# Second batch of an attention-and-Fourier kernel: q and k turned by VectorE, and the block mask added by TensorE

## The chip, the cores and the metric

The kernel runs on one core of one Trainium2 chip. A core has five engines that run their own instruction streams and wait for each other by semaphores: TensorE (matmuls; PE in the profile, its weight loads PEld), VectorE (DVE), ScalarE (ACT), GpSimd (POOL) and SyncE (SP), which here issues most of the transfers. The metric is the device time of one execution in microseconds (us), the median of several runs.

## The reference, cut to what matters

Block-sparse attention for four batches of eight heads, then a Fourier mixing and a two-layer channel network. Everything is float32.

```python
B, H, S, D = 4, 8, 768, 64            # attention
block, n_rand = 32, 3                 # 24 blocks of 32 rows
scores = scale * np.matmul(q, k.transpose(0, 1, 3, 2))
mask = np.abs(blk_i - blk_j) <= 1     # neighbours
mask = mask | first and last block (rows and columns) | three sampled blocks per block row
scores = np.where(mask, scores, -1000000000.0)
attn = softmax(scores);  attn_out = np.matmul(attn, v)
x = attn_out of all heads side by side           # (4, 768, 512)

mixed = np.real(fft(fft(x, axis=1), axis=2))     # Fourier mixing
u = x + mixed
un = (u - mean) / np.sqrt(var + 1e-06)           # per row
out = u + np.maximum(un @ w_ch1, 0.0) @ w_ch2    # channels: 512 -> 2048 -> 512
```

## The kernel before

Two heads form a pair; a batch has four pairs (NP = 4), all batches sixteen, numbered n = 0 to 15. A pair has 12 units (2 halves of the queries times 6 chunks of the keys); a slot handles 2 units, so a pair takes 6 slots and a batch 24 (SB = 24). Slots 0 to 23 are the first batch, 24 to 47 the second, 48 to 71 the third, 72 to 95 the fourth. While a batch's attention runs, the mixing and channels ("mixer") of the batch before it are put into the gaps. The order of instructions on every engine is fixed when the kernel is built, by a small model of the engines' times (`busy`, `when`); on the chip each engine works through its stream in that order.

The scores of a unit have to be masked. The first batch does it on TensorE: a second, bf16 matmul of two small factors (which key block, and which blocks are off for a query) adds a large negative number to the scores in PSUM, so that the exponential is 0. The later batches multiply by a 0/1 mask on VectorE after the exponential. Later batches also have GpSimd add up the exponentials (the row sums), where the first batch uses TensorE.

```python
def scores(us):
    ...
    for u in us:
        s = ps_s.tile([P, 2, 512], FP32, tag="s", name="s")        # 2 buffers in PSUM
        ...
            nc.tensor.matmul(s[:, i, 0:HS], kT[rows, c * P:(c + 1) * P], qT[rows, queries],
                             start=True, stop=n >= NP)
    for u, s in got if n < NP else ():                              # first batch only
        ...
            nc.tensor.matmul(s[:, i, 0:HS], of_k[rows, c * P:(c + 1) * P], off_q[rows, queries],
                             start=False, stop=True)

def weigh(u, s):
    e = ep.tile([P, 2, HS], FP32, tag="e", name="e")                # 4 buffers
    if n < NP:
        nc.scalar.activation(out=e, in_=s[:, :, 0:HS], func=ACT.Exp, scale=scale)
        return
    nc.scalar.activation(out=s[:, :, 0:HS], in_=s[:, :, 0:HS], func=ACT.Exp, scale=scale)
    nc.vector.tensor_tensor(out=e, in0=s[:, :, 0:HS], in1=m.broadcast_to([P, 2, HS]), op=ALU.mult)
    ...
    for i in range(2 if c > 0 else 0):
        nc.gpsimd.tensor_add(out=acc, in0=e_of[u - 1][:, i, :] if c == 1 else acc, in1=e[:, i, :])

def values(u):                          # one slot after its scores
    nc.tensor.matmul(o[D * i:D * i + D, :], vt[:, i, c, :], e[:, i, :], ...)
```

The score matmul needs q and k with the head's dimension on the partitions. Up to pair BY_VECTOR - 1 they are loaded row by row and turned by TensorE into PSUM, from where ScalarE copies them. From pair BY_VECTOR on they are loaded in blocks of 32x32 and turned by VectorE within the blocks; ScalarE then brings the turned q into the order that the mixer needs.

```python
BY_VECTOR = 2 * NP + 1                  # 9

def turn(n, a, half):                   # by TensorE: 6 transposes for k, 6 for q a pair
    nc.tensor.transpose(tp[:, c * P:(c + 1) * P], part, ident)
    ...                                 # then copies on ScalarE

def flip_blocks(n, a):                  # by VectorE
    nc.vector.transpose(out=out, in_=t)

def in_order(n):                        # q only: six copies on ScalarE
    nc.scalar.copy(...)

# in slot(sl), where n, s = divmod(sl, SP): the pair, and its slot from 0 to 5
if s == at and n + 1 < BY_VECTOR: short.append(... turn(n + 1, a, half))
if BY_VECTOR <= n + 1 < len(pairs):
    for at, fn, args in ((0, squares, (n + 1, 0)), (1, flip_blocks, (n + 1, 0)),
                         (2, in_order, (n + 1,)), (4, flip_blocks, (n + 1, 1)),
                         (5, squares, (n + 1, 1))): ...
```

The mixer of a batch: scale x by the row sums, fold it (VectorE), cosine and sine matmuls (zp), matmuls along the other axis (pq), add to x, mean and variance, normalise to un (VectorE), transpose un (utp, TensorE), then the channels: products xp, yp, z of the first layer and y of the second. The channels of a batch are released (`late.extend(rest)`) when everything before them has been put into the streams. In slots 53 and 77 the kernel puts out whatever of the mixer two batches back is still missing (`until`), because x of the new batch takes that batch's buffer.

```python
def begin(b):
    before, after, rest = mixer(b, x_of[b, 0], x_of[b, 1])
    apart.extend((*step, any_of) for step in norm_steps(b) + before)
    apart.extend((*step, hold) for step in after)
    apart.append(("-", lambda: late.extend(rest), 0.0, 0.0, 0.0, hold))

# the weights' raw words pass through six buffers, big0 to big5, which the mixer and
# the channels use afterwards; VectorE converts the last of 32 chunks about slot 23
def room(i, shape, name, dtype=FP32):
    return big.tile(shape, dtype, tag=f"big{i}", name=name)
```

The factors lie in the two buffers of the pool acc_p, which GpSimd's sums take over with the second batch.

Of the kernel before, what the change touches and what calls it, by code (L numbers as in the profile page):

```python
# [12 lines left out]
BF16 = mybir.dt.bfloat16  # L13
# [4 lines left out]
ALU = mybir.AluOpType  # L18
ACT = mybir.ActivationFunctionType
# [83 lines left out]
def kernel(  # L103
# [24 lines left out]
    HS = S // 2  # L128
# [7 lines left out]
    scale = 1.0 / float(D) ** 0.5  # L136
    KA = D + NB
    NP = H // 2
# [27 lines left out]
    mask = const.tile([P, C, S], U8, name="mask")  # L166
# [25 lines left out]
    def busy(engine, us, after=0.0):  # L192
        when[engine] = max(when[engine], after) + us
        return when[engine]
# [11 lines left out]
    HOP = 0.1  # L206
# [2 lines left out]
    loaded, v_of = {}, {}  # L209


    BY_VECTOR = 2 * NP + 1

    def load_blocks(n, a, tile):

# [219 lines left out]
    def room(i, shape, name, dtype=FP32):  # L435
        return big.tile(shape, dtype, tag=f"big{i}", name=name)
# [29 lines left out]

    turned, e_of, acc_of, o_of, sums_of, x_of, sp_of = {}, {}, {}, {}, {}, {}, {}
    s_at, e_at, oT_at, acc_at = {}, {}, {}, {}  # L470

# [64 lines left out]
    def scores(us):  # L536

        n, w = divmod(us[0], UP)
        half = w // C
        qT, kT = turned[n, 0], turned[n, 1]  # L540
        queries = slice(half * HS, (half + 1) * HS)
        got = []
        for u in us:
            c = u % C
            s = ps_s.tile([P, 2, 512], FP32, tag="s", name="s")
            got.append((u, s))
            busy("PE", 0.72, max(e_at.get(u - SLOT, 0.0), z_at[u % 2]))
            s_at[u] = when["PE"] + HOP
            for i in range(2):
                rows = slice(D * i, D * i + D)  # L550
                nc.tensor.matmul(s[:, i, 0:HS], kT[rows, c * P:(c + 1) * P], qT[rows, queries],  # L551
                                 start=True, stop=n >= NP)
        for u, s in got if n < NP else ():
            c = u % C
            busy("PE", 0.25)
            s_at[u] = when["PE"] + HOP
            for i in range(2):
                rows = slice(D * i, D * i + D)
                nc.tensor.matmul(s[:, i, 0:HS], of_k[rows, c * P:(c + 1) * P], off_q[rows, queries],
                                 start=False, stop=True)  # L560
        return got

    def weigh(u, s):
        n, w = divmod(u, UP)
        half, c = divmod(w, C)
        e = ep.tile([P, 2, HS], FP32, tag="e", name="e")
        e_of[u] = e
        if n < NP:
            nc.scalar.activation(out=e, in_=s[:, :, 0:HS], func=ACT.Exp, scale=scale)
            e_at[u] = busy("ACT", 0.8, s_at[u]) + HOP  # L570
            return
        nc.scalar.activation(out=s[:, :, 0:HS], in_=s[:, :, 0:HS], func=ACT.Exp, scale=scale)  # L572
        m = mask[:, c, half * HS:(half + 1) * HS].rearrange("p (o s) -> p o s", o=1)
        nc.vector.tensor_tensor(out=e, in0=s[:, :, 0:HS], in1=m.broadcast_to([P, 2, HS]),  # L574
                                op=ALU.mult)
        e_at[u] = busy("DVE", 0.97, busy("ACT", 0.8, s_at[u]) + HOP) + HOP
        if c > 0:
            acc_at[n, half] = busy("POOL", 2.0, e_at[u]) + HOP
        if c == 1:
            acc_of[n, half] = acc_p.tile([P, 2, HS], FP32, tag="acc", name="acc")  # L580

        for i in range(2 if c > 0 else 0):
            acc = acc_of[n, half][:, i, :]
            nc.gpsimd.tensor_add(out=acc, in0=e_of[u - 1][:, i, :] if c == 1 else acc,  # L584
                                 in1=e[:, i, :])
# [665 lines left out]
    def begin(b):  # L1251


        before, after, rest = mixer(b, x_of[b, 0], x_of[b, 1])
        any_of = len(late) + len(apart) + 4 * len(rest)
        hold = 2 * T
        apart.extend((*step, any_of) for step in norm_steps(b) + before)
        apart.extend((*step, hold) for step in after)
        apart.append(("-", lambda: late.extend(rest), 0.0, 0.0, 0.0, hold))

    def w_loads():
        while state["got"] < min(len(wchunks), state["w"] + ROOMS):
# [3 lines left out]
    def w_steps(sl):  # L1266
        while state["w"] < min(len(wchunks), W_PACE * sl):
            w_round(state["w"])
            state["w"] += 1

    def slot(sl):
        phase, r = divmod(sl, SB)
        n, s = divmod(sl, SP)
        units = range(SLOT * sl, SLOT * sl + SLOT)
        if sl < B * SB:
            for u, ps in scores(units):
                weigh(u, ps)
        if not late:
            gap(1.5)
        if 0 < sl <= B * SB:  # L1280
            done = [u - SLOT for u in units]
            for u in done:
                values(u)
            if phase == 0 or sl == SB:
                add_up(done)
            for u in done:
                e_of.pop(u)
        if s == 3 and n + 2 < len(pairs):
            load_q(n + 2)
        if s == 0 and 0 < n < len(pairs) - 1:  # L1290
            load_k(n + 1)

        reuse = n % NP == 0 and phase >= 2
        if sl > 0 and s == (5 if reuse else 3) and sl <= B * SB:
            b, j = pairs[n]
            at = oT_at[n, 0]
            if reuse:
                until(lambda: (b - 2, 0) in finished)
                at = when["PE"] + LEAVES
            if in_blocks(n):  # L1300
                place_blocks(n, 0)
            else:
                short.append(("t", at, lambda: place(n, 0)))
        if 0 < sl <= B * SB and s == 0 and n % NP != 1:
            if in_blocks(n - 1):
                place_blocks(n - 1, 1)
            else:
                short.append(("t", oT_at[n - 1, 1], lambda: place(n - 1, 1)))
        if sl < B * SB and n % NP == 1 and s == 1:
            b = pairs[n - 1][0]  # L1310
            at = oT_at[n - 1, 1]
            if b >= 2:
                until(lambda: (b - 2, 1) in finished)
# [12 lines left out]
        if sl == 1:  # L1326
            short.append(("t", 0.0, lambda: turn(0, 0, 1)))
        if phase == 0 and 4 <= sl < 4 + 2 * C:
            short.append(("m", 0.0, lambda: mask_step(sl - 4)))
        if r == 1 and 0 < phase:  # L1330
            begin(phase - 1)
        left = SB * (phase + (0 if r == 0 else 1)) + 1 - sl
        us = sum(step[1] for step in late)
        pace = max(LEAST, min(MOST, (us - COVER) / left)) if left > 0 else MOST
        state["owed"] = min(state["owed"], pace) + pace if late else 0.0
        gap(max(state["owed"], 0.0))
        while late and state["owed"] >= late[0][1] / 2:
            state["owed"] -= late[0][1]
            channel_step()
            gap(max(state["owed"], 0.0))  # L1340

        while short and (s in (2, 5) or len(short) > 1 or phase == 0 or r == 0):
            ready = [i for i in short if max(i[1], min(free[i[0]])) <= when["PE"] + 0.1]
            if not ready and s not in (2, 5) and r > 0 and sl > 1:
                break
            item = ready[0] if ready else short[0]
            short.remove(item)
            item[2]()
# [3 lines that stand above are left out]
                                 (5, squares, (n + 1, 1))):  # L1352
                if s == at:
                    fn(*args)
        w_loads()
        w_steps(sl)
        if sl >= 4 and sl % 2 == 0:
            table_step()

# [139 lines left out]
```

## Time and profile before

The time before is 1092.57 us (median of 3 runs, 1092.56 to 1092.97). The profiled execution has a span of 1089.3 us.

| group of instructions | count | mean |
|---|---|---|
| scores on TensorE (s, line 551) | 768 records | 523 ns |
| mask factors on TensorE (s from at_q and at_k, bf16, line 559) | 96 | 323 ns |
| exponential on ScalarE into e (line 569) and in place (line 572) | 48 and 144 | 823 and 791 ns |
| mask multiply on VectorE (e from s and mask, line 574) | 144 | 948 ns |
| sums on GpSimd (acc, line 584) | 240 | 1058 and 1055 ns |
| block transposes on VectorE, of k and of q (line 520) | 7 and 7 | 1524 and 967 ns |
| transposes of q and k on TensorE (tp, line 486) | 108 | 288 to 299 ns |

A float32 matmul shows as two records. Matmuls overlap, so the mean of one record is longer than the time by which it advances the engine; that is read from the starts in the timeline. In the 40 equal slices of the page (27.2 us each) a digit is the busy share in tenths. The second batch's attention falls into slices 5 to 9, where VectorE is at 7 to 9 tenths and GpSimd at 6 to 8:

```profile
PE   8999988988999999999999999999999999999996
...
DVE  5899887598745524664567536554556355575663
ACT  6988655555111102353342202334230302220210
POOL 1000186788000001255555000244530001000000
```

### The profile page before, as it was taken

Reading aid. Unit: us, or ns where it says so; the run is one execution under the profiler, and the core shown is the slowest. Engines: PE = TensorE matmul, PEld = TensorE weight load, DVE = VectorE, ACT = ScalarE, POOL = GpSimd, SP = SyncE. Lnnn points to the kernel's source line nnn. Section 1 sums busy time; section 2 is a strip of 40 time slices with the busy share of each in tenths; the row PEclk is TensorE's granted clock in tenths of the full one; section 3 lists DMA queues with packets and bytes.
Section 4 is the critical chain, followed back from the end, with each engine's and each line's share of the span. In section 5 each row is a group of like instructions: output and inputs, shape, how many; then the busy total and the mean of one; then the engine's idle time right before and its main releaser. Section 6 shows DMA issues by size and latency. Waiting matters only on the chain.

```text
span 1089.3 us, 12419 instructions
## 1 busy us (share of the span) xinstructions
PE 1048.1 (96%) x4334; PEld 534.4 (49%) x4334; DVE 675.3 (62%) x1241; ACT 379.1 (35%) x762; POOL 270.2 (25%) x302
## 2 busy tenths in 40 slices
PE   8999988988999999999999999999999999999996
PEld 4333333533555545443444555443344555568575
DVE  5899887598745524664567536554556355575663
ACT  6988655555111102353342202334230302220210
POOL 1000186788000001255555000244530001000000
PEclk9999999999999999999999999999999999999999
DMA  7757211121000001222311000212000001000001
GB/s 223 229 163 242 78 45 44 30 45 29 0 1 1 0 1 29 59 38 43 56 22 33 0 1 10 63 37 40 13 8 8 1 1 29 30 1 1 1 17 45
DMA packets 108194, 46.66 MB, mean 43 GB/s; under 512 B 95822, under 2 KB 100956, under 8 KB 108124
## 3 DMA queue, kind: packets, MB, share of 16 engines
q1 hardware_dynamic: 106236, 44.99, 16.2%
q10 hardware_dynamic: 1856, 0.79, 0.3%
q8 instruction: 36, 0.59, 0.2%
q14 instruction: 34, 0.28, 0.1%
q0 software_dynamic: 32, 0.01, 0.0%
HBM read 37.11 MB, written 6.29 MB: 40 GB/s over the span
## 4 chain that ended last, share of the span: by engine, by line
PE 83%; DVE 9%; ACT 3%; issue 2%; DMA 2%; POOL 1%; SPq 0%; ACTq 0%; DVEq 0%; POOLq 0%
PE y L1048 23%; PE z L992 15%; PE s L551 10%; PE o L597 8%; PE yp L992 7%; PE yy L1111 6%; PE xp L992 3%; DVE e L574 3%; PE zp L805 2%; PE sp L663 1%; PE zp L776 1%; DMA out_dram<-x 1%; DVE x L855 1%; POOL acc L584 1%; PE tp L486 1%
## 5 line engine op out<-in xcount | busy, mean ns | idle before, releaser
L584 POOL TENSOR_TENSOR acc<-acc,e 128x384 f32<-128x384 f32 x192 | 196.8, 1058 | 83.8 <-DVE e L574 83.2
L551 PE MATMUL s<-qT,kT 64*128 64x384 f32 x768 | 157.4, 523 | 13.9 <-DVE e L574 12.1
L574 DVE TENSOR_TENSOR e<-s,mask 128x768 f32<-128x768 f32 x144 | 131.1, 948 | 58.6 <-ACT s L572 53.3
L572 ACT ACTIVATE s<-s 128x768 f32<-128x768 f32 x144 | 109.6, 791 | 112.1 <-PE s L551 111.1
L597 PE MATMUL o<-e,vr 128*64 128x384 f32 x768 | 145.5, 500 | 0.0
L1051 DVE TENSOR_TENSOR x<-y,x 128x512 f32<-128x512 f32 x72 | 49.7, 690 | 139.4 <-PE y L1048 139.3
L1048 PE MATMUL y<-w_sb,hA 128*128 128x512 f32 x288 | 129.8, 597 | 1.1 <-ACT zs L807 1.1
L1048 PE MATMUL y<-w_sb,hB 128*128 128x512 f32 x288 | 128.7, 597 | 1.0 <-DVE x L1051 1.0
L551 PEld LDWEIGHTS s<-qT,kT 64*128 64x128 f32 x768 | 63.7, 187 | 89.7 <-DVE e L574 43.1
L584 POOL TENSOR_TENSOR acc<-e 128x384 f32<-128x384 f32 x48 | 49.6, 1055 | 219.6 <-DVE e L574 170.3
L997 DVE TENSOR_TENSOR hA<-z,hA 128x384 f32<-128x384 f32 x64 | 35.7, 557 | 96.3 <-PE z L992 96.3
L992 PE MATMUL z<-unT,t 128*128 128x384 f32 x256 | 93.0, 486 | 0.0
L868 POOL TENSOR_SCALAR st<-st 128x1 f32<-128x1 f32 x24 | 6.6, 276 | 347.0 <-DVE st L867 346.5
L1048 PEld LDWEIGHTS y<-w_sb,hB 128*128 128x128 f32 x288 | 53.3, 190 | 68.5 <-issue 66.5
L1048 PEld LDWEIGHTS y<-w_sb,hA 128*128 128x128 f32 x288 | 52.9, 190 | 64.8 <-issue 58.3
L597 PEld LDWEIGHTS o<-e,vr 128*64 128x64 f32 x768 | 46.8, 137 | 76.3 <-issue 71.1
L1001 ACT ACTIVATE hA<-hA 128x384 f32<-128x384 f32 x64 | 33.5, 523 | 120.1 <-DVE hA L997 119.9
L992 PEld LDWEIGHTS z<-unT,t 128*128 128x128 f32 x256 | 48.6, 190 | 33.9
L1001 ACT ACTIVATE hB<-hB 128x384 f32<-128x384 f32 x64 | 33.5, 523 | 86.3 <-DVE hB L997 86.3
L1012 ACT COPY hA<-xp 128x384 f32<-128x384 f32 x32 | 15.3, 478 | 100.0 <-PE xp L992 100.0
L992 PE MATMUL xp<-unT,w_sb 128*128 128x384 f32 x128 | 48.9, 505 | 1.3 <-DVE x L1051 0.7
L992 PE MATMUL yp<-unT,w_sb 128*128 128x384 f32 x128 | 46.9, 489 | 0.4 <-DVE un L841 0.4
(200 smaller groups left out, 1388.1 us busy)
## 6 DMA issues: line engine op xcount, KB each, us to landing
wraw<-in_moe_w_ch_dram SPq DMA_DIRECT2D x32, 512.0 KB
vr<-in_v_dram SPq DMA_DIRECT2D x30, 192.0 KB
qr<-in_q_dram SPq DMA_DIRECT2D x48, 64.0 KB
x<-oT SPq DMA_DIRECT2D x192, 12.0 KB
kr<-in_k_dram SPq DMA_DIRECT2D x14, 192.0 KB
qb<-in_q_dram SPq DMA_DIRECT2D x28, 96.0 KB
kb<-in_k_dram SPq DMA_DIRECT2D x28, 96.0 KB
out_dram<-x SPq DMA_DIRECT2D x16, 128.0 KB
```

The lines of the kernel that those rows point to most:

```text
L551: nc.tensor.matmul(s[:, i, 0:HS], kT[rows, c * P:(c + 1) * P], qT[rows, queries], start=True, stop=n >= NP)
L572: nc.scalar.activation(out=s[:, :, 0:HS], in_=s[:, :, 0:HS], func=ACT.Exp, scale=scale)
L574: nc.vector.tensor_tensor(out=e, in0=s[:, :, 0:HS], in1=m.broadcast_to([P, 2, HS]), op=ALU.mult)
L584: nc.gpsimd.tensor_add(out=acc, in0=e_of[u - 1][:, i, :] if c == 1 else acc, in1=e[:, i, :])
L597: nc.tensor.matmul(o[D * i:D * i + D, :], vt[:, i, c, :], e[:, i, :], start=(c == 0), stop=(c == C - 1))
L805: nc.tensor.matmul(ps[:, 0:KS - 1], sd[:, t, parts[g - 2]], sn_sb[:, t, :], start=(t == 0), stop=(t == T - 1))
L992: nc.tensor.matmul(to, a[:, k, :], c[:, k, :], start=(k == 0), stop=(k == ND // 2 - 1))
L997: tt(out=to, in0=ps, in1=a, op=ALU.add)
L1001: nc.scalar.activation(out=h, in_=h, func=ACT.Relu)
L1048: nc.tensor.matmul(y, hs[0, half][:, l, m * P:(m + 1) * P], w2_sb[:, 4 * r + l, :], start=(l == 0), stop=(l == 3))
L1051: nc.vector.tensor_tensor(out=x[:, m, :], in0=y, in1=x[:, m, :], op=ALU.add)
L1111: nc.tensor.matmul(ps, a[:, k, :], c[k // 2][:, k % 2, :] if isinstance(c, list) else c[:, k, :], start=(k == 0), stop=(k == 3))
```

## The change

The change has two parts that belong together.

First, VectorE turns q and k from pair 5 on (the sixth pair) instead of from pair 9 on: `BY_VECTOR` becomes NP + 1. This takes transposes from TensorE and copies from ScalarE.

Second, units of the second batch are masked by TensorE's two factors, as those of the first batch are, so that VectorE has no multiply to do for them; this lasts until the channels of the first batch are released, because the factors are kept in a buffer (big2) that the channels need. The factors are copied there by two transfers in slot 21. GpSimd's sums stay as they are.

```diff
-    BY_VECTOR = 2 * NP + 1
+    BY_VECTOR = NP + 1
...
+    by_pe = set()
+    factors = {"at": (of_k, off_q)}
+
+    def keep_factors():
+
+        kept = room(2, [P, 2, S], "factors", BF16)
+        for a, t in enumerate(factors["at"]):
+            nc.sync.dma_start(out=kept[:, a, :], in_=t)
+        factors["at"] = kept[:, 0, :], kept[:, 1, :]
...
+            if n < NP or (factors["at"] and True):
+                by_pe.add(u)
...
-                                 start=True, stop=n >= NP)
-        for u, s in got if n < NP else ():
-            c = u % C
+                                 start=True, stop=u not in by_pe)
+        for u, s in got:
+            if u not in by_pe:
+                continue
+            c, (at_k, at_q) = u % C, factors["at"]
...
-                nc.tensor.matmul(s[:, i, 0:HS], of_k[rows, c * P:(c + 1) * P], off_q[rows, queries],
+                nc.tensor.matmul(s[:, i, 0:HS], at_k[rows, c * P:(c + 1) * P], at_q[rows, queries],
                                  start=False, stop=True)
...
-        if n < NP:
+        if u in by_pe:
             nc.scalar.activation(out=e, in_=s[:, :, 0:HS], func=ACT.Exp, scale=scale)
             e_at[u] = busy("ACT", 0.8, s_at[u]) + HOP
+        else:
+            ...                          # exponential in place and multiply, as before
+        if n < NP:
             return
...
-        apart.append(("-", lambda: late.extend(rest), 0.0, 0.0, 0.0, hold))
+
+        def go():
+            late.extend(rest)
+            factors["at"] = None
+        apart.append(("-", go, 0.0, 0.0, 0.0, hold))
...
+        if sl == SB - 3:
+            keep_factors()
```

Because the build-time model sees other durations, the scheduler also places the mixer's steps in other slots, in the second batch and in later ones.

More of the change, by code (lines that the diff above doesn't have):

```diff
@@ L567, in weigh @@
         e_of[u] = e
-        if n < NP:
+        if u in by_pe:
             nc.scalar.activation(out=e, in_=s[:, :, 0:HS], func=ACT.Exp, scale=scale)
             e_at[u] = busy("ACT", 0.8, s_at[u]) + HOP
-            return
[L572 to L576, printed above, removed]
+        else:
+            nc.scalar.activation(out=s[:, :, 0:HS], in_=s[:, :, 0:HS], func=ACT.Exp, scale=scale)
+            m = mask[:, c, half * HS:(half + 1) * HS].rearrange("p (o s) -> p o s", o=1)
+            nc.vector.tensor_tensor(out=e, in0=s[:, :, 0:HS], in1=m.broadcast_to([P, 2, HS]),
+                                    op=ALU.mult)
+            e_at[u] = busy("DVE", 0.97, busy("ACT", 0.8, s_at[u]) + HOP) + HOP
+        if n < NP:
+            return
         if c > 0:
```

## The prediction

> **What bounds the kernel now.** I read the page first (busy shares), then the chain of waits, then TensorE's waits, then windows cut at the kernel's own stages, and last the timeline where those windows showed idle time.
>
> ```profile
> PE 1048.1 (96%) x4334; PEld 534.4 (49%) x4334; DVE 675.3 (62%) x1241; ACT 379.1 (35%) x762; POOL 270.2 (25%) x302
> PE 83%; DVE 9%; ACT 3%; issue 2%; DMA 2%; POOL 1%; SPq 0%; ACTq 0%; DVEq 0%; POOLq 0%
> PE s L551 <- DVE e L574: 12.1, 11, 2.5
> ...
> PE utp L917 <- DVE un L880: 3.1, 1, 3.1
> ```
>
> TensorE is busy for 1048.1 of 1089.3 us and carries 83% of the chain; all that a schedule can win is its 41.2 us of idle time. The largest named wait is of scores (s) for the VectorE multiply that makes e (line 574). The windows say where it lies. I cut at slot starts, found in the timeline as the starts of the score matmuls: slot 24 (second batch begins) at 122.8, slot 48 at 242.0.
>
> ```profile
> 122.80:242.00 119.20, 105.68 (x569) 46.56 (x568) 90.97 (x127) 65.75 (x142) 84.21 (x82) 0.97 0.17 41
> 242.00:281.00 39.00, 33.98 (x162) 16.34 (x163) 32.22 (x48) 18.11 (x33) 27.29 (x31) 0.96 0.16 31
> 281.00:441.50 160.50, 159.58 (x497) 83.71 (x497) 81.75 (x168) 30.50 (x65) 5.36 (x12) 1.00 0.03 7
> 441.50:688.00 246.50, 244.66 (x911) 115.44 (x909) 143.61 (x238) 75.38 (x145) 86.57 (x92) 1.00 0.15 30
> 688.00:816.00 128.00, 125.10 (x500) 55.82 (x500) 70.63 (x108) 46.15 (x82) 57.91 (x60) 1.00 0.15 30
> 816.00:1089.00 273.00, 262.42 (x931) 166.90 (x927) 153.49 (x312) 42.05 (x88) 5.20 (x12) 0.99 0.05 13
> ```
>
> After the length, each row gives busy us of PE, PEld, DVE, ACT and POOL. From 122.8 to 281 TensorE idles 13.52 + 5.02 = 18.5 us; from 281 to 816, where channel matmuls fill the slots, only 0.9 + 1.8 + 2.9. So the stage the change touches holds nearly half of the idle time, and VectorE, 78% busy there (123.2 of 158.2), is its cause. The same stage has a second loss, the granted clock:
>
> ```profile
> 129.02:132.43 3.41, 3.10 (x10) 1.37 (x12) 2.16 (x4) 0.91 (x2) 1.94 (x2) 0.50 0.00 0
> 183.64:187.05 3.41, 3.41 (x13) 1.44 (x13) 2.82 (x6) 2.07 (x3) 0.00 (x0) 0.50 0.00 0
> 268.97:272.38 3.41, 3.41 (x9) 2.20 (x8) 3.38 (x3) 0.66 (x2) 3.32 (x3) 0.50 0.02 5
> ```
>
> ```profile
> 129.33 2.93 PE L551 MATMUL s<-qT,kT 64*128 64x384 f32 x8 [2.27 <-DVE e L574]
> 182.94 2.51 PE L551 MATMUL s<-qT,kT 64*128 64x384 f32 x8 [2.48 <-DVE e L574]
> 268.78 0.93 PE L917 MATMUL utp<-ident,un 128*128 128x128 f32 x4 [3.12 <-DVE un L880]
> ```
>
> Three times a wait of 2.3 to 3.1 us is followed by a stretch of 3.41 us at half clock, in which the same eight score matmuls take 2.93 instead of 1.56 us. Half of 3.41 is lost each time, 3 x 1.7 = 5.1 us. It counts as busy, so it stands beside the 18.5.
>
> **What the Trainium skill says.** "TensorE: Matmul & The Clock Gate", What's actually happening: the array's clock drops to half after about one idle window of 3.4 us. The three rows above agree in length and in the 0.50, though here waits of 2.3 to 3.1 us were enough. "SBUF — State Buffer", SBUF: two separate sides: VectorE and GpSimd share one port pair; a VectorE instruction with two SBUF inputs and a GpSimd one block each other. The trace agrees: the adds on GpSimd (acc) take 983 ns at least, 998 in the median, 2527 at most; the scaling of x (two SBUF inputs) has a mean of 1063 ns in this stage against 0.68 us where no add runs beside it. The mask multiply has one input in PSUM and stays at 912 to 958 ns. So taking it away relieves VectorE, not GpSimd. "VectorE: DVE Perf Modes", The three transpose paths: VectorE transposes 32x32 blocks only, which is why q and k must then be loaded in blocks.
>
> **The change part by part.** The order of the instructions in both programs gives the counts.
>
> *Mask in the second batch.* 42 units (slots 24 to 44 of the second batch's 24 to 47) lose the VectorE multiply: 42 x 0.948 = 39.8 us of VectorE. Each gets two bf16 matmuls; four of them (a slot) advance TensorE by 0.43 us in the first batch's timeline (19.36 to 19.79), so 21 slots x 0.43 = +9.0 us of TensorE. The hop from ScalarE to VectorE to TensorE becomes one from ScalarE, 0.95 us shorter.
>
> *Turning pairs 5 to 8.* Removed: 48 transposes on TensorE at 0.16 us (three advance it by 0.48): -7.7 us. Added on VectorE: 4 x (1.524 + 0.967) = +10.0 us. ScalarE changes 2 copies of k (0.48) and nine small ones of q for six of q: about -1.5 us a pair, off the path. Bytes loaded are equal, in pieces of 128 B instead of 256 B, at a DMA share of 0.17: hidden.
>
> *Keeping the factors.* Two copies of 192 KB, wanted at slot 22 (113.2 + 1.4 us). Their buffer is free when weight chunk 26 is converted, at 110.3; the issues follow four of q at about 112.5. With a landing about 2 to 3 us later I allow +0.7 us of waiting.
>
> Net TensorE work: +9.0 - 7.7 + 0.7 = +2.0 us. VectorE in the stage: -29.8 of 123.2 us.
>
> *What moves.* The scheduler now puts the first Fourier matmuls at slot 31 instead of 37, and channels start at slot 45 instead of in slot 53, where both programs work off the rest. Moving work wins nothing by itself; it matters in filling idle slots.
>
> How much of the 18.5 + 5.1 = 23.6 us is recovered? Three stretches remain. Slots 24 to 33: TensorE's slot is now 1.39 (scores) + 0.43 + 1.44 (values) + about 0.3 (transposes of o and sums) = 3.55 us. GpSimd needs 20 adds a pair, at the 1.097 us this stage shows, 21.9 us in six slots or 3.66 a slot: as long as TensorE. And VectorE must there scale x (6 x 1.06), fold (15 us in the timeline from 156 to 185), turn two pairs (5.0) and finish two weight chunks, some 33 us in about 30. So slot 30 (first score on a VectorE-turned k) and slot 31 (cosines on the folds) will wait, together about 4 us, and one stretch of half clock is likely (1.7). Slots 34 to 44: TensorE has the Fourier matmuls besides, about 4.7 us a slot; 2 us idle. Slots 45 to 53: the masks are back on VectorE but channels fill; 2 us. Left over: 4 + 2 + 2 + 1.7 = 9.7; recovered 23.6 - 9.7 = 13.9 us.
>
> *Given back later.* From slot 77 the order differs again. Before, slots 79 to 95 alternate channels and bare slots, and idle is 2.9 us (688 to 816). After, the last transposes of un lie in slots 81 to 89, so the third batch's channels start only in slot 89 and are heaped into 91 to 94. Nine slots, 80 to 88, are bare: per slot TensorE 2.93 (bare slot 49: 248.42 to 251.35) + 0.4, GpSimd 20 x 1.05 / 6 = 3.5 (1.05 us is the mean of the adds from 460 to 600), VectorE two multiplies (1.9) plus 13.4 us over nine slots = 3.4. Three engines level, chained through two score buffers: I take 3.8 to 3.9 us a slot, so 9 x 0.5 = 4.5 us idle where about 0.5 of the present 2.9 falls away: +4 us.
>
> Sum: 1092.6 + 2.0 - 13.9 + 4.0 = 1084.7 us.
>
> **The rivals.**
> - *All idle time goes.* Slots 24 to 53 become bound by TensorE. For it: waits for e (line 574) are 10.0 of the 18.5 us, and the first batch, with the same factors, runs at 39 of 40 us busy. Against it: GpSimd's 3.66 a slot, which the first batch doesn't have, and the folds. It would give 1092.6 + 2.0 - 23.6 + 4 = 1075.
> - *GpSimd or the folds become the bound.* If the adds and folds meet more often now that both run closer together, adds at 1.25 us make a slot of 4.2 us, 0.65 idle over ten slots, with more half-clock stretches; recovery falls to 6 or 7 us: about 1092.
> - *The tail eats it.* If bare slots 80 to 88 run as the second batch does now (119.2/24 = 5.0 us a slot, some of it transposes) the loss is 9 to 10 us with a half-clock stretch: 1090 to 1092, nearly no change.
>
> **Range and chances.** What the stage holds at most is 23.6 - 2.0 = 21.6 us, and 2% is 21.9 us: a fall of over 2% would need idle time won elsewhere too. A rise of 2% would need new waits of over 40 us. I predict 1084 us, with 1075 (first rival) and 1093 (second or third) as the range.
>
> **What would show it.** Right: the multiply (line 574 before) counts 102 instead of 144; TensorE's waits for it from 122 to 281 fall below 4 us; the stretch before slot 54 is about 14 us shorter; waits of scores for kT and of zp for folds appear near 146 to 155; idle from slot 79 to 95 rises from 2.9 to about 7 us; GpSimd's adds stay near 1.1 us. Wrong: TensorE idle over 14 us from slot 24 to 53; a wait of several us for the factors at slot 22; more than two half-clock stretches; or a change outside slots 22 to 95.

## The result: 2.2% slower, and the profile after

The changed kernel takes 1117.78 us (median of 4 runs, 1116.6 to 1119.03) where the kernel before takes 1092.77 us beside it; the ratio is 1.0224, 95% interval [1.0205, 1.0242]. The prediction was 1084 us with a range from 1075 to 1093, so it missed, and in the wrong direction. The profiled execution has a span of 1115.7 us, 26.4 us more than before.

The page of the changed kernel comes first: busy us by engine, and the shares of the chain of waits.

```profile
PE 1052.4 (94%) x4370; PEld 535.0 (48%) x4370; DVE 666.4 (60%) x1207; ACT 375.4 (34%) x742; POOL 278.6 (25%) x302
...
PE 83%; DVE 8%; DMA 3%; ACT 2%; SPq 2%; issue 2%; POOL 0%; DVEq 0%; ACTq 0%; POOLq 0%
```

Then TensorE's waits: for each pair of waiting line and releaser the total us, the number of waits and the longest.

```profile
PE s L565 <- DVE e L590: 10.1, 8, 3.1
PE s L565 <- DVE kT L532: 8.8, 1, 8.8
PE utp L935 <- ACT x L638: 7.0, 1, 7.0
PE utp L935 <- DVE sums L665: 6.3, 1, 6.3
PE s L575 <- DMA factors<-at_q: 3.5, 1, 3.5
```

TensorE's idle time has grown from 41.2 to 63.3 us (span less busy time). Four single waits that the kernel before doesn't show make 25.6 us: 8.8 for a k turned by VectorE, 7.0 for a copy of x by ScalarE, 6.3 in the normalisation and 3.5 for the factors. The chain still gives TensorE 83%: a share of the chain hides four waits that together are 2.3% of the span.

The next fence has the windows of the changed kernel cut at its own slot starts: slots 22, 24, 29, 31, 37, 40, 54, 79 and 95. After the length, each row has busy us of PE, PEld, DVE, ACT and POOL, the granted clock, the DMA share and GB/s.

```profile
113.06:127.94 14.88, 11.33 (x66) 4.16 (x66) 11.01 (x24) 8.17 (x14) 0.00 (x0) 0.89 0.21 45
127.94:146.92 18.98, 18.98 (x122) 8.28 (x121) 14.55 (x26) 12.93 (x25) 13.65 (x12) 1.00 0.34 64
146.92:165.49 18.57, 9.79 (x51) 3.96 (x49) 15.72 (x16) 4.87 (x9) 12.35 (x9) 0.72 0.13 21
165.49:200.05 34.56, 34.56 (x202) 18.23 (x199) 13.46 (x24) 18.01 (x39) 21.06 (x22) 1.00 0.21 44
200.05:221.49 21.44, 13.60 (x77) 5.51 (x76) 12.47 (x21) 8.63 (x18) 12.24 (x15) 0.85 0.08 16
221.49:446.36 224.87, 217.85 (x793) 108.12 (x791) 124.03 (x216) 61.54 (x122) 62.48 (x69) 0.99 0.08 15
446.36:703.60 257.24, 252.08 (x942) 117.36 (x941) 144.33 (x227) 81.30 (x157) 83.54 (x84) 1.00 0.16 31
703.60:820.42 116.82, 103.00 (x424) 44.26 (x420) 71.93 (x103) 38.68 (x67) 60.26 (x64) 0.97 0.14 29
```

The loss stands in a few rows. Slots 22 and 23 take 14.88 us (9.56 before) and idle 3.55. Slots 24 to 28 run without any idle time, as hoped. Slots 29 and 30 take 18.57 us, of which TensorE is busy for 9.79, and at a mean clock of 0.72; before they took 7.52. Slots 37 to 39 idle 7.84 us, and slots 79 to 94 idle 13.8 where the same sixteen slots idled 2.90.

The stretches at half clock, in windows again:

```profile
119.69:123.10 3.41, 3.41 (x15) 0.71 (x12) 1.98 (x4) 0.86 (x2) 0.00 (x0) 0.50 0.00 0
153.82:164.06 10.24, 5.04 (x18) 2.39 (x20) 8.86 (x13) 2.45 (x4) 5.45 (x5) 0.50 0.24 38
215.26:222.09 6.83, 4.41 (x14) 2.00 (x16) 6.67 (x13) 4.14 (x10) 5.74 (x7) 0.50 0.29 48
331.30:334.71 3.41, 3.41 (x12) 1.09 (x12) 1.96 (x3) 1.58 (x2) 3.29 (x4) 0.50 0.22 34
723.85:730.68 6.83, 3.92 (x14) 1.61 (x14) 1.40 (x2) 4.04 (x10) 0.00 (x0) 0.50 0.22 48
```

Half of the busy time in such a stretch is lost: 20.19 / 2 = 10.1 us, where the three stretches before lost 9.92 / 2 = 5.0. What is left of busy time when this is taken off I call work at full clock: 1052.4 - 10.1 = 1042.3 us after, 1048.1 - 5.0 = 1043.1 before. So the 26.4 us of the span are 22.1 of idle time, 5.1 of half clock and -0.8 of work. The net work was foreseen; everything that went wrong is waiting.

Last, the timeline at the four waits: start, length, engine, line, operation, count, and in brackets the idle time before it and what ended it.

```profile
118.23 0.50 PE L575 MATMUL s<-factors 64*128 64x384 bf16 x4 [3.55 <-DMA factors<-at_q]
...
139.78 7.87 DVE L723 TENSOR_TENSOR x<-x,r 128x512 f32<-128x512 f32 x6
147.06 12.21 POOL L602 TENSOR_TENSOR acc<-acc,e 128x384 f32<-128x384 f32 x8
147.68 2.44 DVE L746 TENSOR_TENSOR sa<-x 128x1536 f32<-128x1536 f32 x1
...
157.38 1.49 DVE L532 STREAM_TRANSPOSE kT<-kb 128x768 f32<-128x768 f32 x1
...
159.02 1.65 PE L565 MATMUL s<-qT,kT 64*128 64x384 f32 x4 [8.78 <-DVE kT L532]
...
206.62 1.95 POOL L602 TENSOR_TENSOR acc<-e 128x384 f32<-128x384 f32 x2 [7.83 <-PE sp L695]
...
209.57 1.21 DVE L898 TENSOR_SCALAR un<-x,st 128x512 f32<-128x512 f32 x1 [8.12 <-POOL st L888]
...
217.68 1.12 PE L935 MATMUL utp<-ident,un 128*128 128x128 f32 x4 [6.27 <-DVE sums L665]
...
726.22 0.48 ACT L638 COPY x<-xt 128x384 f32<-128x384 f32 x1 [9.73 <-DMA out_dram<-x]
...
726.75 1.11 PE L935 MATMUL utp<-ident,un 128*128 128x128 f32 x4 [7.00 <-ACT x L638]
```

Read from 139.78 on. VectorE scales x, six instructions in 7.87 us (1.31 from one to the next; 0.68 where no sum runs beside it), while GpSimd adds. VectorE's folds follow; beside them GpSimd takes 12.21 us for eight additions (1.53 each; 0.98 at least in the kernel before). Behind six of the folds in VectorE's stream stands the turning of k of the sixth pair. It starts at 157.38, and the scores of slot 30 have waited 8.78 us for it. The third wait, of 6.27 us, begins on GpSimd: two additions wait there 7.83 us for TensorE's row sums (sp), GpSimd's step of the normalisation (st) stands behind them, and VectorE waits 8.12 us for that step before it can make un. The fourth wait is one of a transfer: at 726.22 ScalarE has waited 9.73 us for the output of the second batch to leave the buffer of x, and TensorE behind it 7.00 us.

### The profile page after: what moved, and what is told of

Same layout as the page of the kernel before. It is cut to its first block, busy times and chain, and to the rows that moved or that the text cites. A ratio compares the mean times of both kernels' runs of the same rounds, so it can differ in the third digit from the quotient of the medians.

```text
span 1115.7 us, 12397 instructions
## 1 busy us (share of the span) xinstructions
PE 1052.4 (94%) x4370; PEld 535.0 (48%) x4370; DVE 666.4 (60%) x1207; ACT 375.4 (34%) x742; POOL 278.6 (25%) x302
## 4 chain that ended last, share of the span: by engine, by line
PE 83%; DVE 8%; DMA 3%; ACT 2%; SPq 2%; issue 2%; POOL 0%; DVEq 0%; ACTq 0%; POOLq 0%
PE y L1066 22%; PE z L1010 15%; PE s L565 10%; PE o L615 9%; PE yp L1010 7%; PE yy L1129 6%; PE xp L1010 4%; SPq L653 2%; PE zp L823 1%; DVE x L723 1%; DMA out_dram<-x 1%; PE sp L681 1%; PE s L575 1%; PE zp L794 1%; DVE e L590 1%
## 5 line engine op out<-in xcount | busy, mean ns | idle before, releaser
L602 POOL TENSOR_TENSOR acc<-acc,e 128x384 f32<-128x384 f32 x192 | 204.6, 1099 | 99.8 <-DVE e L590 91.1
L565 PE MATMUL s<-qT,kT 64*128 64x384 f32 x768 | 155.9, 521 | 21.8 <-DVE e L590 10.1
L615 PE MATMUL o<-e,vr 128*64 128x384 f32 x768 | 150.2, 514 | 2.2 <-DVE oT L622 2.2
L590 DVE TENSOR_TENSOR e<-s,mask 128x768 f32<-128x768 f32 x102 | 92.6, 947 | 50.5 <-ACT s L588 49.5
L588 ACT ACTIVATE s<-s 128x768 f32<-128x768 f32 x102 | 77.3, 790 | 127.9 <-PE s L565 127.1
L602 POOL TENSOR_TENSOR acc<-e 128x384 f32<-128x384 f32 x48 | 50.6, 1075 | 270.3 <-ACT e L585 131.8
L585 ACT ACTIVATE e<-s 128x768 f32<-128x768 f32 x90 | 68.1, 813 | 32.7 <-PE s L575 28.3
L1010 PE MATMUL z<-t,w_sb 128*128 128x384 f32 x128 | 46.8, 488 | 1.9 <-DVE t L972 1.9
```

The source lines that it names most:

```text
L1010: nc.tensor.matmul(to, a[:, k, :], c[:, k, :], start=(k == 0), stop=(k == ND // 2 - 1))
```

## The experiments

The theory after the result: the build-time model fixes orders in which VectorE's stream is late wherever GpSimd adds beside it, and late in the program an order in which a transfer has no time; both are orders, not work. The rivals: the work itself is too much for VectorE once it turns q and k; or the factors' copy is what costs.

### The two parts alone, and a later switch to the copy

Turning alone keeps `BY_VECTOR = NP + 1` and leaves the mask multiply on VectorE for the second batch:

```diff
-            if n < NP or (factors["at"] and True):
+            if n < NP:
                 by_pe.add(u)
```

> Only the turning by VectorE from pair 5 on; all masks of the second batch stay on VectorE, no factors are copied. Theory A (the change loses where VectorE's and GpSimd's queues are late, and the turning puts TensorE behind them): VectorE gets 10 us more in its fullest stage and nothing is taken from it, so TensorE's idle time from slot 24 to 53 rises from 18 to 22 or more, which eats the 7.7 us of transposes: 1090 to 1097 us. Rival B (the mask by TensorE is the guilty half, the turning is a gain): about 1085 us.

Measured: 1103.88 us, ratio 1.0087 [1.0063, 1.0112]. Idle time 53.3 us, lost to half clock 14.9, work at full clock 1034.7. So turning does take 8.4 us of work from TensorE (7.7 predicted), and the waits take more than that back: scores wait 19.7 us for VectorE's masked e, and the transposes of un 11.1 us for VectorE's un.

Masking alone:

```diff
-    BY_VECTOR = NP + 1
+    BY_VECTOR = 2 * NP + 1
```

> Only the mask by TensorE in the second batch; TensorE turns q and k of pairs 5 to 8 as before. Theory A: 9.0 us more matmuls, some 5 us for the late factors at slot 22, no wait of scores for a kT made by VectorE, 10 to 15 us of idle time and half clock recovered, and the order from slot 78 on is that of the kernel before, so nothing is lost there: 1088 to 1097 us. Rival B: about 1117 us, as the whole change.

Measured: 1090.51 us, ratio 0.9962 [0.9945, 0.9978]. Idle time falls to 34.3 us, work rises by 4.8. It still waits 3.4 us for the factors. The two parts alone give +0.9% and -0.4%; together they give +2.2%. The rest, some 1.7% or 19 us, belongs to neither part but to how the schedule with both comes out.

The whole change, with slots 22 and 23 still masked from the first batch's own factors, and the copy used from slot 24 on:

```diff
-        factors["at"] = kept[:, 0, :], kept[:, 1, :]
+        factors["kept"] = kept[:, 0, :], kept[:, 1, :]
...
+        if sl == SB:
+            factors["at"] = factors["kept"]
```

> The whole change, but slots 22 and 23 still use the factors' old buffers and the copies are first used in slot 24. Theory A: the wait of 3.5 us in slot 22 and the stretch of half clock behind it (1.7 us) go, 5 us less than the change: 1112 us. Rival C (what waits in slot 22 is only shifted, because VectorE and not TensorE decides when slot 31 can go on): slot 30 waits 5 us longer for kT and the time stays at 1117 us.

Measured: 1113.1 us, ratio 1.0178 [1.0157, 1.02]. Slots 22 and 23 are back at 9.56 us, the wait for the factors is gone, and the wait for kT is 8.8 us again. The other stages stay within 0.7 us, but for slots 84 to 89, which take 1.6 us more with a half-clock stretch in them. The factors' copy was worth 5.3 us of slots 22 and 23, and is not the main cause.

The same switch with masking alone:

> The mask by TensorE alone (turning by VectorE only from pair 9 on) and the copied factors first used in slot 24. Theory A: the 3.4 us wait and the half clock of slot 22 go from the mask-only kernel's 1090.5: 1085 to 1086 us, faster than both kernels. Rival C: the wait moves to slot 30 or 31, where the cosines wait for the folds: 1090 us.

Measured: 1081.9 us, ratio 0.9896 [0.9879, 0.9912]: faster than both kernels. Its largest remaining wait in the stage is 3.6 us of the first cosine matmul (zp) for VectorE's folds in slot 30, with a half-clock stretch of 6.83 us around its end.

### Slots 29 to 45: what makes VectorE late

The whole change, with GpSimd's additions of the second batch left out but for the first of each half, so that the row sums of that batch are incomplete:

```diff
-        for i in range(2 if c > 0 else 0):
+        for i in range(2 if c == 1 or (c > 0 and n // NP != 1) else 0):
```

> The whole change, but GpSimd leaves out the sums of the second batch except the first addition of each half (64 of 80 additions; the row sums of that batch are then incomplete). Same order of TensorE's instructions. Theory D (GpSimd's additions and VectorE's two-input instructions hold each other up, and that makes kT and the folds late): the scaling of x falls from 1.31 to about 0.7 us each and the folds from 16 to 10 us, the wait for kT in slot 30 falls from 8.8 to under 2 us, the wait of utp behind the sums in slot 39 goes: 1098 to 1105 us. Rival E (VectorE's queue is simply too long there): the wait for kT stays above 6 us and the time above 1110 us.

Measured in one run: 1103.25 us. TensorE's waits in this kernel, as above:

```profile
PE s L565 <- DVE e L590: 10.0, 8, 3.1
PE utp L935 <- ACT x L638: 6.9, 1, 6.9
PE utp L935 <- DVE sums L665: 3.9, 1, 3.9
```

and its timeline where the changed kernel waits for kT:

```profile
139.56 3.70 DVE L723 TENSOR_TENSOR x<-x,r 128x512 f32<-128x512 f32 x6
...
149.93 1.48 DVE L532 STREAM_TRANSPOSE kT<-kb 128x768 f32<-128x768 f32 x1
...
151.55 1.56 PE L565 MATMUL s<-qT,kT 64*128 64x384 f32 x8 [1.52 <-DVE kT L532]
```

The wait for kT falls from 8.8 to 1.5 us and so drops out of the list's head; slots 29 and 30 take 8.9 instead of 18.6 us. VectorE's instructions and their order are the same (1207 of them), yet its busy time on the page falls from 666.4 to 646.0 us. The scaling takes 3.70 instead of 7.87 us, and the six folds ahead of k 6.64 (143.29 to 149.93) instead of 9.70: together 7.2 us, which is the fall of the wait. So most of that wait is not VectorE's own work but the work drawn out by sums running beside it. In slots 37 to 39 the idle time falls from 7.84 to 4.58 us. VectorE still waits 8.13 us there for GpSimd's step of the normalisation, behind the same two additions, which this kernel keeps. So 4.58 us of that loss remain without the contention, behind the order of GpSimd's stream.

The late switch with k of the sixth pair turned two slots earlier, ahead of the folds in VectorE's stream; TensorE's order is unchanged:

```diff
-                                 (2, in_order, (n + 1,)), (4, flip_blocks, (n + 1, 1)),
+                                 (2, in_order, (n + 1,)),
+                                 (2 if n == NP else 4, flip_blocks, (n + 1, 1)),
```

> The whole change with the factors first used in slot 24, and VectorE turns k of pair 5 two slots earlier, before most of the scaling and the folds; TensorE's order is the same. Theory F (VectorE's queue between slot 26 and 31 is too long, whatever stands first in it): the wait of 8.8 us for kT goes but 6 to 7 us come back before the cosines in slot 31: 1109 to 1113 us. Rival G (only the place of the k transposition was wrong): 8.8 us and the half clock after it are won: 1101 to 1103 us.

Measured: 1110.17 us, ratio 1.016 [1.0143, 1.0177]. The wait for kT is gone, and TensorE's list of waits has a new line:

```profile
PE sp L695 <- POOL acc L602: 3.9, 1, 3.9
```

Slot 29 takes 3.26 us, slot 30 10.59: together 13.85 instead of the 19.16 of the late switch. It wasn't the cosines that waited next, as I had thought, but the row sums' matmul (sp) for GpSimd's own additions, which run against the folds. Moving one consumer exposes the next: the pair of engines is late as a whole.

### Slots 79 to 95: the transfer behind the copy

The whole change, with the output transfers of the second batch's second half left out (those rows of the output are not written):

```diff
-            for p0, cnt, rows in _rows(out[b], T * half + m):
+            for p0, cnt, rows in () if (b, half) == (1, 1) else _rows(out[b], T * half + m):
```

> The whole change without the output transfers of the second half of batch 1 (those 384 rows are not written). Same order. Theory H (in slot 80 ScalarE waits for these transfers before it may overwrite x, and TensorE stands behind it): the 7.0 us wait of utp for ScalarE and the half clock behind it go: 8 to 11 us less than the change, 1106 to 1110 us. Rival I (bare slots are slow by themselves): 1115 us or more.

Measured in one run: 1109.67 us. Slots 79 to 83 as a window (in the changed kernel 703.60 to 737.67):

```profile
704.30:729.71 25.41, 24.38 (x116) 10.30 (x112) 21.55 (x33) 12.03 (x22) 18.05 (x22) 1.00 0.12 20
```

They take 25.41 instead of 34.07 us, their idle time falls from 7.94 to 1.03, and their half-clock stretch is gone. The other stages agree with the changed kernel within 0.4 us. So the wait of 7.0 us at 726.75 is the transfer's. In the kernel before, SyncE begins to issue those outputs at 693.87 and ScalarE's first copy into that buffer comes at 715.27 without waiting; in the changed kernel the issue begins at 707.69 and ScalarE is ready for the copy at 716.49 (726.22 - 9.73).

The whole change with the last batch's x moved by one transfer of 192 KB a half instead of sixteen of 12 KB. The values then land in another order within the rows, with the same bytes moved:

```diff
+        if b == 3:
+            nc.sync.dma_start(out=x_of[b, half][:, :, j * P:(j + 1) * P],
+                              in_=oT.rearrange("p c t d -> p c (t d)"))
+            return
         for g in range(P // BLK):
```

> The whole change, but in the last batch each half's output of attention goes into x with one transfer of the same bytes instead of sixteen (32x32 blocks stay unswapped, so the values are in wrong places). Same order. Theory J (SyncE needs 0.64 us per issue, 42 issues a pair = 27 us, and bare slots take less, so the queue holds the single buffer oT back): the waits of values for oT and part of the waits for e between slot 84 and 90 go, 3 to 5 us less than the change: 1112 to 1115 us. Rival I: no difference.

Measured in one run: 1115.03 us. The waits of values for oT in slots 84 to 89, 1.9 us, are gone, and idle time there falls from 5.01 to 2.86 us, but the stage only from 35.39 to 34.58, as a half-clock stretch lies in it now. With such a stretch the late switch idles 3.71 us there as well, and a kernel with sixteen issues and the same late order (f = 1.8 below) 2.88. So what the sixteen issues (SyncE needs 0.64 us for each) cost TensorE isn't shown.

### The order alone

If the orders are at fault and not the work, then the same work in another order must be fast. The model takes VectorE's scaling of x and its folds at fixed durations. For the first batch's mixer these were multiplied by a factor f, here 2.0:

```diff
-                [("d", lambda h=h, c=c: scale_x(h, c), 0.0, 0.0, 0.9)
+                [("d", lambda h=h, c=c: scale_x(h, c), 0.0, 0.0, 1.8 if b == 0 else 0.9)
...
+        if b == 0:
+            first = [(k, fn, pe, act, 2.0 * us) for k, fn, pe, act, us in first]
```

No instruction changes by this, only where the scheduler puts it and, a little, which units the factors mask. With a larger f the first cosines come in a later slot, and with the whole change k of the sixth pair is turned ahead of the folds. The channels of the first batch are then released a little later, so that a few more units are masked by the factors: in the whole change 84 of their matmuls with f = 1, 100 with 1.8 and 104 with 2.0; with masking alone 76, 88 with 1.6 and 96 with 2.0. f = 2.0 isn't the true slowdown (the scaling in the model is 0.9 us, in the trace 1.31); it is a way to get other orders.

Masking alone with f = 1.6:

> The late-switched masks alone (1081.9 us), with the first batch's scaling of x and its folds entered in the build-time model at 1.6 times their former durations, as the traces show them beside GpSimd's sums; the first cosines then stand after slot 32's other work instead of in slot 30. Theory (the model's durations, which know nothing of the contention, put the cosines before their folds are there): the wait of zp for the folds in slot 30 (3.6 us) and the half-clock stretch behind it go, 3 to 5 us less: 1077 to 1079 us. Rival (VectorE and GpSimd have the same work, so the wait only moves to the next consumer, as it did when k was turned first): within 1.5 us of 1081.9.

Measured: 1097.21 us, ratio 1.0033 [1.0022, 1.0044], which neither theory nor rival had. The wait of zp did go: slot 30 takes 7.78 instead of 15.03 us. But the order after it changed as well, and against masking alone with f = 1 the idle time rises from 30.1 to 37.0 us and work by 2.7: scores wait 3.6 us for a masked e once in slots 48 to 52, and further half-clock stretches come in slots 54 to 78 and after slot 95. A wait removed in one stage was paid for in three others.

Masking alone with f = 2.0:

> As the run before it with a factor of 2.0; first cosines in slot 34, the order of the late batches as in the kernel before. Theory: the wait of zp is gone as well, but the mixer starts a slot or two later and leaves the slots before it bare: 1077 to 1081 us. Rival: slots 24 to 33 are then limited by GpSimd's sums at 3.7 us a slot and more, and what the wait cost comes back there: 1082 us or more.

Measured: 1083.34 us, ratio 0.9905 [0.9885, 0.9925], the same as with f = 1 within the intervals. That is where the rival put it, but not for the rival's reason: in slots 24 to 33 TensorE idles 2.6 us, and 4.8 with f = 1. Idle and lost time fall (30.1 to 28.9 and 6.5 to 1.7 us) and work rises by 4.0, of which the 20 additional factor matmuls are about 2.1 (0.43 for four).

The whole change, late switch, f = 1.8:

> The whole change with the factors first used in slot 24 (1113.1 us), and the first batch's scaling of x and folds entered in the model at 1.8 times: k of pair 5 is then turned right after the scaling, before the folds, and the first cosines stand in slot 34. The order from slot 79 on is still that of the changed kernel. Theory (two independent losses: orders around slot 30 that the contention upsets, and the heaped late channels): the early loss falls by 10 us or more and the late one of about 16 us stays: 1098 to 1104 us. Rival (with VectorE turning q and k there is too much for VectorE and GpSimd in slots 24 to 45, whatever the order): within 4 us of 1113.

The whole change, late switch, f = 2.0:

> As the run before it with a factor of 2.0, whose one large difference is that the order from slot 79 on is again that of the kernel before. Theory: slots 79 to the end take 10 to 16 us less than in the run before it, so 1085 to 1092 us in all; the same whole change is then no slower than the kernel before. Rival (the late loss comes from the work itself and not from its order): the two runs agree within 3 us.

Measured: 1108.19 us with 1.8, ratio 1.0126 [1.0105, 1.0146], and 1083.1 us with 2.0, ratio 0.9896 [0.9871, 0.9922]. The first lies between what the theory and the rival said: the early loss fell by less than thought. The second is below what the theory said, and it settles the question: the whole change in another order is 1% faster than the kernel before and 2.8% faster than with f = 1 (0.9896 / 1.0178). The page's busy line of this kernel:

```profile
PE 1048.3 (97%) x4390; PEld 534.7 (49%) x4390; DVE 655.8 (61%) x1197; ACT 376.1 (35%) x742; POOL 275.4 (25%) x302
```

and its windows, cut at slots 24, 29, 31, 37, 54, 79 and 95 (without 54 to 78):

```profile
122.88:141.86 18.98, 18.98 (x121) 8.27 (x120) 16.97 (x29) 12.92 (x25) 14.20 (x12) 1.00 0.33 64
141.86:152.48 10.62, 8.95 (x50) 3.17 (x49) 4.17 (x3) 5.41 (x10) 10.62 (x10) 1.00 0.35 74
152.48:180.51 28.03, 28.03 (x161) 13.45 (x160) 17.74 (x16) 15.45 (x31) 21.51 (x20) 1.00 0.22 44
180.51:419.88 239.37, 232.46 (x913) 118.04 (x913) 141.25 (x245) 72.62 (x146) 75.47 (x84) 0.99 0.07 14
...
684.11:793.54 109.43, 106.87 (x429) 46.78 (x428) 61.23 (x94) 39.65 (x70) 48.32 (x50) 1.00 0.15 31
```

Slots 29 and 30 take 10.62 us where the changed kernel takes 18.57, and slots 79 to 94 idle 2.56 us where it idles 13.8.

Up to the start of slot 30 the traces of the two runs agree within 0.1 us; then one difference shows the contention by itself. In both, VectorE turns k at 142.5, then does the first fold. With f = 1.8 two more folds follow at once; with f = 2.0 VectorE does nothing for 6.56 us. VectorE's and then GpSimd's timeline, f = 1.8:

```profile
142.47 1.53 DVE L532 STREAM_TRANSPOSE kT<-kb 128x768 f32<-128x768 f32 x1
143.85 2.14 DVE L746 TENSOR_TENSOR sa<-x 128x1536 f32<-128x1536 f32 x1
145.91 2.55 DVE L746 TENSOR_TENSOR sd<-x 128x1536 f32<-128x1536 f32 x1
148.38 1.74 DVE L750 TENSOR_TENSOR sa<-sa 128x765 f32<-128x765 f32 x1
...
141.97 11.86 POOL L602 TENSOR_TENSOR acc<-acc,e 128x384 f32<-128x384 f32 x8
```

and f = 2.0:

```profile
142.51 1.53 DVE L532 STREAM_TRANSPOSE kT<-kb 128x768 f32<-128x768 f32 x1
143.89 2.14 DVE L746 TENSOR_TENSOR sa<-x 128x1536 f32<-128x1536 f32 x1
152.59 0.56 DVE L663 COPY sums<-sp 128x384 f32<-128x384 f32 x1 [6.56 <-PE sp L695]
...
142.01 9.66 POOL L602 TENSOR_TENSOR acc<-acc,e 128x384 f32<-128x384 f32 x8
```

The same eight additions take 11.86 us beside three folds and 9.66 us beside one: two folds of 4.29 us put 2.2 us on GpSimd, and TensorE's wait for its sums is 3.8 against 1.6 us. It pays not to start a fold there, although VectorE is free. Over the whole stage the fast order has no less of this contention: its fourteen folds take 17.7 us together (14.4 in the changed kernel), and the 80 additions of the batch 1.14 us on average in both. What differs is who stands behind: k is turned ahead of the folds, and the first cosines come in slot 35 instead of 31.

Where the 27 us of span between the two profiled executions lie:

| stage | f = 1.8 | f = 2.0 | idle + lost, 1.8 | idle + lost, 2.0 |
|---|---|---|---|---|
| slots 22 to 53 | 322.34 | 306.56 | 22.4 | 10.3 |
| slots 54 to 78 | 260.27 | 264.23 | 8.6 | 5.4 |
| slot 79 to the end | 411.78 | 396.61 | 26.8 | 14.0 |

From slot 79 on, 15.2 us, of which 12.8 are idle and lost time and 2.4 are work that the other order has done before. The instructions of the two kernels differ in two multiplies and four factor matmuls only. That is the late order alone; slots 79 to 94 take 109.43 us as in the kernel before (109.78). The rival, that the late loss is the work's, falls.

All runs with a trace and several timings, in us of the profiled execution:

| kernel | ratio | idle | lost at half clock | work at full clock |
|---|---|---|---|---|
| before | 1 | 41.2 | 5.0 | 1043.1 |
| the change | 1.0224 | 63.3 | 10.1 | 1042.3 |
| turning alone | 1.0087 | 53.3 | 14.9 | 1034.7 |
| masking alone | 0.9962 | 34.3 | 4.8 | 1047.9 |
| masking alone, late switch | 0.9896 | 30.1 | 6.5 | 1047.2 |
| the same, f = 1.6 | 1.0033 | 37.0 | 7.8 | 1049.9 |
| the same, f = 2.0 | 0.9905 | 28.9 | 1.7 | 1051.2 |
| the change, late switch | 1.0178 | 58.1 | 12.5 | 1041.4 |
| the same, k first | 1.016 | 53.3 | 10.7 | 1043.2 |
| the same, f = 1.8 | 1.0126 | 49.8 | 13.7 | 1044.1 |
| the same, f = 2.0 | 0.9896 | 32.4 | 3.4 | 1044.9 |

## Why the prediction was wrong, point by point

The span rose by 26.4 us where a fall of 7.9 was predicted. Of these 34.3 us, 21.4 lie in slots 22 to 53 (-11.9 predicted, +9.5 measured) and 12.3 from slot 79 on (+4 predicted, +16.3 measured). What failed are the term of 13.9 us recovered, with its waits in slots 22 to 53, and the term of 4 us given back later.

*Net TensorE work, +2.0 us, 0.7 of it waiting.* Right: work at full clock changed by -0.8 us against +1.3 predicted. Turning alone takes 8.4 us away (7.7). The multiply counts 102 instances instead of 144, as predicted, and TensorE waits only 2.0 us for it from slot 24 to 53.

*Keeping the factors, +0.7 us.* Wrong by the size of the term: 5.3 us. The four issues of q before them took 3.39 us of SyncE, so the factors' issues, put at about 112.5 us, began at 113.55 and ended at 114.72, and they landed 3.5 us later, not 2 to 3. Slot 22 then idled 3.55 us, and a half-clock stretch took another 1.7. I had named a wait of several us there as a sign against me; it came, and the late switch removes it.

*Slots 24 to 33, "together about 4 us, and one stretch of half clock is likely (1.7)".* The first five slots were right (18.98 / 5 = 3.80 us each, 3.55 to 3.66 expected, no idle time). Of the two waits only the first came, in slot 30, and it was mis-sized: 8.8 us and 2.5 lost. The cosines of slot 31 didn't wait; slots 31 to 33 have no idle time. The step that failed is "some 33 us in about 30" for VectorE. The sum was right: VectorE is busy for 32.2 us in slots 24 to 33. But a balance over ten slots doesn't say when each piece can start and is needed. The scaling can't start before the reciprocals of the row sums are there, at 139.74, and slot 30 was ready for its k at 150.24. Into these 10.5 us fall the scaling, six folds and the turning of k, 19.1 us as they ran. With the durations that the kernel before shows for the same instructions it would be 15.8 us, a wait of 5.3 (an estimate). The rest is contention: the scaling takes 1.31 instead of 1.06 us, and the six folds 9.7 us instead of 7.9. In the kernel before, scaling, multiplies and folds lie spread between 139 and 185 us; the change packs them together, beside GpSimd's additions. The mechanism itself stands in the prediction, from "SBUF — State Buffer", SBUF: two separate sides, of the Trainium skill; the runs agree with it (eight additions in 11.86 us beside three folds and 9.66 beside one, and the wait for kT of 8.8 us falling to 1.5 without the additions). But it was used only to say that taking away the multiply "relieves VectorE, not GpSimd"; what VectorE does in the time won, fold with two SBUF inputs against GpSimd, was left to the second rival. GpSimd's additions did "stay near 1.1 us" on average (1.14).

*Slots 34 to 44, 2 us, and 45 to 53, 2 us.* Measured 9.8 idle and 2.2 lost, then 5.1 and 1.7 (4.2 of the idle time in slots 48 to 52). The 6.3 us in slot 39 are the normalisation's chain, which runs through VectorE and GpSimd by turns, with GpSimd's part queued behind additions that had waited 7.83 us for TensorE; I had not traced it. (Ahead of the prediction VectorE is put at 7 to 9 tenths during the second batch; one of these slices, from 190.6 to 217.9 us, has 5, so VectorE wasn't the limit throughout.)

*Recovered, 13.9 of 23.6 us.* From slot 22 to 53 the idle and lost time went from 24.4 to 35.3 us instead.

*Given back later, "+4 us".* Right in place and direction, wrong in size: from slot 79 to the end +16.3 us, of which 13.3 are idle and lost time and 3.0 work moved there. I reckoned with three engines level at 3.8 to 3.9 us a slot and looked at no transfer. The output of the second batch, now issued just ahead of the copy that needs its buffer, made 7.0 us of it and a half-clock stretch; leaving the transfers out recovers 8.7. "The tail eats it" named 9 to 10 us there, from the wrong cause.

*Slots 54 to 78* idled 3.3 us more, which I had not foreseen; nothing was run on it alone.

*Range.* "A rise of 2% would need new waits of over 40 us" was wrong arithmetic. 21.9 us are 2%, and I had added to them the gains that I believed in. The real waits were 22.1 us, and the clock 5.1. The second rival, GpSimd or the folds as the bound, was the right mechanism with too small a figure (about 1092), and the second and third came together, which no case of mine added up.

What stays open: what makes slots 84 to 89 idle; and why turning adds nothing in time to the best order without it. Masking alone and the whole change end level (both 0.9896): with f = 2.0, turning takes 6.3 us of work away and puts 3.5 of idle and 1.7 of lost time in its place, so the sums are known but not the cause.

## What to carry to other kernels

In a kernel whose order is fixed by a model, a change of durations or of engines is a change of order: compare orders stage by stage, and try the same work in another order before judging the work (here 31 us of span). When one engine is nearly full, don't only balance its sum over a stage: set what stands ahead of each consumer against the time between its earliest start and its need (here 19.1 us against 10.5, while the sum over the stage was right). Take the durations for a prediction from rows in which the same neighbours run; where freed time will be filled by instructions that slow a neighbour, size both at their slow durations. And follow each transfer that frees a buffer to its next writer, and ask how many us lie between its issue and that writer now.

## What the runs showed of the hardware that I had not expected

A long wait brings more than one half-clock stretch of 3.41 us: those at the waits of 8.8, 6.3 and 7.0 us last 10.24, 6.83 and 6.83 us (three and two times 3.41). Where one turns into two isn't sharp here: the wait of 3.55 us in slot 22 has 3.41, that of 3.64 us with masking alone and the late switch 6.83. Part of each long stretch lies in the wait itself, which is why only 2.5, 2.2 and 2.0 us are lost.

GpSimd's additions and VectorE's instructions with two SBUF inputs slow each other: the scaling goes from 0.68 to 1.31 us beside additions, the additions from 0.98 to 1.53 beside folds. And leaving VectorE idle for 6.56 us made the program's next step come 2.5 us sooner (slot 31 starts at 152.48 instead of 155.01).

Small transfers cost their issue: SyncE needs 0.64 us for each of 12 KB, and 0.60 to 0.71 for one of 192 KB. Two copies of 192 KB within the chip landed some 3.5 us after the second was issued.
